# Attention blocks of 58 queries by 64 keys in batches 0 and 1, with v loaded by single heads

## The chip, the cores and the metric

The kernel runs on one core of a Trainium2 chip. The metric is the device time of one execution in microseconds (us). Several executions of a kernel are compared by their median.

## The reference

The program is an attention layer followed by a feed-forward layer. Attention has a local part, in which a position sees the keys less than four positions away, and a pooled part over averages of four positions:

```python
q_d = q.reshape(B, H, Sd, 4, D).mean(axis=3)          # B, H, S, D = 8, 8, 576, 64; Sd = 144
out_d = sm_attn(q_d, k_d, v_d)                        # softmax attention over all 144 averages
out_up = np.repeat(out_d, 4, axis=2)
mask = np.abs(pos[:, None] - pos[None, :]) < 4
scores = np.where(mask, scale * q @ k.T, -1e9)
attn_out = out_up + softmax(scores) @ v
x = attn_out.transpose(0, 2, 1, 3).reshape(4608, 512)
h = x @ w_in                                          # w_in: 512 x 2048
out = np.where(h > 0, h, np.exp(np.minimum(h, 0)) - 1) @ w_out
```

All inputs and the output are float32; the kernel's matmul operands are fp16.

## The kernel before

The eight batches each have four pairs of heads. A batch gives 576 of the 4608 rows of x, and the feed-forward layer works in nine blocks of 512 rows, so its block 0 needs batch 0 alone and block 1 needs batches 0 and 1.

For each pair (load, cast, transposes, scores, weigh): q and k come by DMA as float32, are cast to fp16 on DVE, POOL or ACT, and are transposed on TensorE by a matmul against an identity, with the averages of four beside them. DVE or ACT evicts the result into qt, kt and kd. In batches 0 and 1 (SIX) six neighbouring tokens lie in one partition, and k of some pairs comes as fp16 straight into a tile kc by a GpSimd DMA. In the other batches each partition holds one token of each 96-token block.

Local scores are made in small tiles. A block of 96 queries is two halves of KB = 48 queries, each against a window of KR = 64 keys; six blocks cover the 576 positions. Four such tiles (two halves, two heads) run in the four quarters of TensorE's array. One group for a pair is 24 of these matmuls (line 757) and 12 of 64 by 72 for the pooled scores. In batch 0 the mask is added by a matmul of NEG (line 763), in the others the exponentials are multiplied by MASK on DVE (line 792). ACT takes the exponential of a pair in one instruction (line 787).

The sums of the exponentials (denominators, line 810) are inverted by DVE (line 828) and spread over the partitions. In batches 0 and 1 (BY_PE) TensorE does that with a selection matrix (line 841) and DVE or ACT evicts it into rcb (line 850). In the others GpSimd writes them to DRAM and reads them back (lines 855 and 860).

v is loaded by load_v into the same windows: 64 partitions for each half, 48 blocks of 64 floats, in two DMAs per half (line 568; one of batch 0's by ACT, the others by SP). It is cast to fp16 (line 572) and pooled by matmuls (line 722 in batch 0, line 705 in the others), which are evicted into vd. The outputs (line 883) are again small tiles of 64 by 48 and 64 by 72. DVE normalizes them into xn (lines 910 and 914), and DVE or POOL adds the local and the repeated pooled part into xt (line 933), which is the x that the feed-forward layer reads.

In the feed-forward layer mm1 (line 950) makes 16 tiles of h for a block of 512 rows, four matmuls each. ACT and DVE apply the activation (lines 956, 958 and 961). mm2 (line 979) makes four output tiles in four parts each, ACT evicts them (line 995) and SP stores them (line 997). The weights come in eight parts by GpSimd DMAs (line 606).

The order is made in the kernel's Python. Each operation has an engine, an assumed duration and a rank. The class Plan plays these on the engines, gives out buffers and PSUM banks, and lets an engine take the ready operation of the lowest rank. The program is then written in that order, and every engine executes its own list strictly in order. The ranks come from the tables PARAM and FIRST, and PARAM also chooses engines (its e_ entries). WGATE and LGATE name an operation that a weight part, or a load of batch 1, waits for; the tiny memsets at line 1041 are these gates. While TensorE would stand idle early on, the plan inserts matmuls on a tile of zeros (fill, line 357). Eight semaphores serve the DMAs of SP and ACT in turn, so the ninth DMA waits for the first to land.

Of the kernel before, what the change touches and what calls it, by code (L numbers as in the profile page):

```python
# [12 lines left out]
AB = mybir.AluOpType  # L13
# [3 lines left out]
SD = S // 4  # L17
# [7 lines left out]
NR = 10  # L25
# [15 lines left out]
BY_PE = (0, 1)  # L41
WIC = (0, 512, 1024, 1536, 2048)
# [22 lines left out]
class Plan:  # L65
# [197 lines left out]
    def emit(self):  # L263
        for o in self.order:
# [8 lines left out]
PARAM = dict(e_d0=2, e_d1=0, e_d2=0, e_d3=1, M0=27.21, P=36.34, LAG=0.71, LEAD=52.25, GAP=6.32, SC=5.0,  # L273
             DEN=30.8, OUT=1.3, OUTG=2.09, LOAD=15.53, VLOAD=34.45, VCAST=9.57, warm=3.4, FILL=36.0, WI=-28.49,
             WO=59.77, WOG=5.01, OVER=1.64, LEAD1=58.97, GAP1=6.47, OUT1=55.0, VLOAD1=29.88, LOAD1=41.47,
             CC=-34.39, tv0=-22.07, C0=-2, SC0=3.1, OUTA=-23.54, OUTB=-20, DEN0=2.92, DENB=-27.58, SPA=-26.75,
             SPB=-20.86, V0=-43, G0=0, G1=0, G2=0, G3=2, G4=12, G5=6, G6=12, G7=3, G8=13, L0=0, L1=1, L2=2,
             L3=4, L4=4, LAG0=0.75, BY4=-51.82, TV1=0.68, C1=-19.87, e_cq0=0, e_cq1=1, e_cq2=1, e_cq3=1,
             e_ck0=0, e_ck1=0, e_ck2=1, e_ck3=1, e_q0=1, e_q1=0, e_q2=0, e_q3=0, e_k0=1, e_k1=1, e_k2=0,
             e_k3=0, QG=2.5, tvA=-26, e_v0=2, e_v1=1, e_v2=2, e_v3=1, e_g0=1, e_g1=1, e_g2=1, e_g3=1, e_r0=1,  # L280
             e_r1=0, e_r2=1, e_r3=1, e_xr0=0, e_xr1=1, e_xr2=0, e_xr3=1, e_a0=1, e_a1=0, e_a2=1, e_a3=0,
             e_xq0=1, e_xq1=0, e_xq2=1, e_xq3=0, e_xk0=1, e_xk1=0, e_xk2=1, e_xk3=1, KS=-64, KSG=3, e_s0=0,
             e_s1=1, e_s2=1, e_s3=0, e_xs0=0, e_xs1=1, e_xs2=1, e_w0=0, e_w1=1, e_w2=0, e_w3=0, e_xs3=0)

FIRST = {
    "add000": 0.72, "add001": 3.11, "add010": 0.8, "add011": 1.42, "add020": -0.47, "add030": 1.32,
    "add031": 0.68, "cast000": 0.77, "cast011": 1.41, "cast021": 4.15, "cast030": 0.71, "den00": -0.64,
    "den02": -0.88, "evk00": 0.17, "evk01": -0.98, "evk03": 0.21, "evq00": -5.46, "evq01": -5.01,
    "evq03": 0.38, "evr01": -3.98, "evr02": -2.25, "evv01": 6, "evv02": -2.4, "evv03": 0.21, "ex00": -5.19,
    "ex01": 5.05, "ex02": 0.83, "ex03": -1.67, "load00k": -4.99, "load01k": -2.41, "mask1": 6, "mask6": -3.11,  # L290
    "out00": -0.66, "out01": 4.25, "out02": -0.47, "out03": 1.13, "recip02": -2.47, "sc01": 0.78,
    "sc03": -0.22, "select": -0.15, "sixths": -1.87, "spr00": -2.79, "spr01": -3.25, "spr02": -1.4,
    "spr03": -1.43, "tens": 0.56, "tk00": -5.07, "tk01": -0.72, "tk02": 3.96, "tk03": 1.15, "tq00": 3.92,
    "tq01": 0.71, "tq02": -1.94, "tv00": -4.97, "vb": 1.68, "vc00": 2.37, "vc01": -3.26, "vc02": -4.17,
    "xn00": -1.03, "xn01": -5.03, "xn02": -0.06,
# [4 lines left out]
def kernel(  # L300
# [15 lines left out]
    def many(kind, shape, dt=FP16):  # L316
# [8 lines left out]
        "qt": many("qt", [128, 720]),  # L325
        "kt": many("kt", [128, S + 16]),
        "ex": many("ex", [128, 2, EW]),
        "vd": many("vd", [128, 3, NPAIR, 128]),
        "rcb": many("rcb", [128, NPAIR, 2, GW]),
        "rc": many("rc", [128, HD]),  # L330
        "xn": many("xn", [128, 2 * GW]),
# [32 lines left out]
    def const(name, shape):  # L364
# [4 lines left out]
        "BY6": const("BY6", [QB, NB, SD]),  # L369
        "VR": const("VR", [128, 32]),  # L370
        "VB": const("VB", [128, 28]),
        "BND": const("BND", [128, KR + KB]),
        "MASK": const("MASK", [128, NB, KB]),
        "NEG": const("NEG", [128, NB, KB]),
        "FIRST": const("FIRST", [128, 32]),
        "PICK": const("PICK", [128, 2, 51]),
        "EYE": const("EYE", [128, 128]),
# [718 lines left out]
```

## Time and profile before

| | |
|---|---|
| median of three runs | 349.6 us (348.94 to 353.46) |
| the profiled execution | 349.04 us |
| its span, first to last instruction | 347.3 us |
| granted TensorE clock, mean | 0.984 |
| instructions | 10965 |
| first feed-forward matmul | 34.12 us |

A profile's groups have this form: line, engine and operation, destination <- source, shape, count, then the busy time, the mean of one in ns, and the idle time before them with the releaser that ended most of it. In a timeline, a line has the start, the duration, the engine and the count, and in brackets the idle time ahead of it and what ended it. PEld is the loading of weights into TensorE, which runs beside its matmuls. "issue" is time for which the profile names no wait. The page's slices are fortieths of the span, 8.7 us each, and each digit is a busy share in tenths.

### The profile page before, as it was taken

Reading aid. Unit: us, or ns where it says so; the run is one execution under the profiler, and the core shown is the slowest. Engines: PE = TensorE matmul, PEld = TensorE weight load, DVE = VectorE, ACT = ScalarE, POOL = GpSimd, SP = SyncE. Lnnn points to the kernel's source line nnn. Section 1 sums busy time; section 2 is a strip of 40 time slices with the busy share of each in tenths; the row PEclk is TensorE's granted clock in tenths of the full one; section 3 lists DMA queues with packets and bytes.
Section 4 is the critical chain, followed back from the end, with each engine's and each line's share of the span. In section 5 each row is a group of like instructions: output and inputs, shape, how many; then the busy total and the mean of one; then the engine's idle time right before and its main releaser. Section 6 shows DMA issues by size and latency. Waiting matters only on the chain.

```text
span 347.3 us, 10965 instructions
## 1 busy us (share of the span) xinstructions
PE 331.9 (96%) x4672; PEld 172.4 (50%) x4672; DVE 218.0 (63%) x459; ACT 196.4 (57%) x337; POOL 132.6 (38%) x190
## 2 busy tenths in 40 slices
PE   6967999999999999899989999999999999999995
PEld 3744564555554455445544455545554444444443
DVE  6564788467474986377756786577657738655530
ACT  3582577297754686277817762776376325444431
POOL 6583133765449443732455246623410150000000
PEclk9896999999999999999999999999999999999999
DMA  8999999999999999999957995003100310001011
GB/s 204 208 213 243 195 191 205 176 192 233 223 186 202 237 227 224 178 244 216 192 131 141 189 202 137 32 32 87 64 32 30 90 64 30 32 30 60 32 54 67
DMA packets 120196, 49.73 MB, mean 143 GB/s; under 512 B 106996, under 2 KB 114708, under 8 KB 120148
## 3 DMA queue, kind: packets, MB, share of 16 engines
q1 hardware_dynamic: 112004, 39.33, 58.1%
q0 software_dynamic: 6592, 9.32, 14.5%
q8 instruction: 36, 0.59, 0.8%
q10 hardware_dynamic: 1552, 0.39, 0.6%
q14 instruction: 12, 0.10, 0.1%
HBM read 44.27 MB, written 9.55 MB: 155 GB/s over the span
## 4 chain that ended last, share of the span: by engine, by line
PE 58%; issue 0%; ACT 0%; DVE 0%; ACTq 0%
PE bank L979 27%; PE bank L950 24%; PE bank L662 2%; PE bank L883 2%; PE bank L757 1%; PE bank L705 1%; PE bank L810 1%; ACT os L995 0%; DVE xn L914 0%; ACTq L995 0%
## 5 line engine op out<-in xcount | busy, mean ns | idle before, releaser
L979 PE MATMUL bank<-WO,gt 128*128 128x512 f16 (+1 forms) x592 | 141.5, 374 | 1.5 <-DVE xn L914 1.2
L950 PE MATMUL bank<-xt,WI 128*128 128x512 f16 x576 | 141.6, 380 | 0.5 <-DVE gt L961 0.5
L956 ACT ACTIVATE e<-bank 128x512 f16<-128x512 f32 x144 | 86.8, 604 | 62.0 <-PE bank L950 45.1
L958 DVE TENSOR_SCALAR e<-e 128x512 f16<-128x512 f16 x144 | 58.0, 406 | 72.7 <-ACT e L956 72.5
L961 DVE SCALAR_TENSOR_TENSOR gt<-bank,e 128x512 f16<-128x512 f32 x144 | 98.6, 689 | 5.2
L979 PEld LDWEIGHTS <-gt 128*128 128x128 f16 x592 | 55.1, 98 | 60.4 <-DVE xn L914 1.7
L950 PEld LDWEIGHTS <-WI 128*128 128x128 f16 x576 | 53.5, 98 | 61.2 <-issue 2.9
L625 POOL CAST c<-ld 96x768 f16<-96x768 f32 x54 | 44.7, 839 | 34.5 <-issue 15.2
L933 POOL TENSOR_TENSOR xt<-xn 128x64 f16<-128x64 f16 (+7 forms) x62 | 40.4, 678 | 40.6 <-DVE xn L914 40.5
L995 ACT COPY os<-bank 128x512 f32<-128x512 f32 (+1 forms) x37 | 21.2, 575 | 40.9 <-PE bank L979 40.7
L910 DVE TENSOR_TENSOR xn<-bank,rcb 128x576 f16<-128x576 f32 x32 | 24.1, 753 | 22.0 <-POOL xt L933 9.8
L787 ACT ACTIVATE ex<-bank 128x1008 f16<-128x1008 f32 x32 | 31.6, 1010 | 8.3 <-PE bank L757 8.3
L572 POOL CAST v<-v 128x768 f16<-128x768 f32 x30 | 24.7, 848 | 23.1 <-DMA v<-in_v_dram 11.6
L677 ACT CAST qt<-bank 128x720 f16<-128x720 f32 x24 | 18.3, 763 | 18.6 <-PE bank L662 18.5
L662 PEld LDWEIGHTS <-c 96*128 96x128 f16 x288 | 18.9, 97 | 10.2 <-POOL c L625 0.5
L662 PE MATMUL bank<-ONE,c 96*128 96x120 f16 x288 | 22.1, 216 | 0.0
L855 POOL DMA_DIRECT2D rd<-rc x6 | 3.5, 579 | 47.2 <-DVE rc L828 44.7
L689 ACT CAST kt<-bank 128x576 f16<-128x576 f32 x24 | 15.8, 658 | 2.3 <-PE bank L662 2.3
L792 DVE TENSOR_TENSOR ex<-ex,MASK 128x576 f16<-128x576 f16 x28 | 14.9, 536 | 3.4 <-ACT ex L787 3.4
L883 PEld LDWEIGHTS <-v 64*64 64x64 f16 x768 | 9.4, 111 | 9.2 <-issue 9.1
L883 PE MATMUL bank<-ex,v 64*64 64x48 f16 x768 | 11.8, 191 | 1.8 <-issue 1.8
L757 PEld LDWEIGHTS <-kt 64*64 64x64 f16 x768 | 9.0, 109 | 8.0 <-issue 6.3
(90 smaller groups left out, 218.5 us busy)
## 6 DMA issues: line engine op xcount, KB each, us to landing
v<-in_v_dram SPq DMA_DIRECT2D x29, 384.0 KB, 7.7
ld<-in_q_dram SPq DMA_DIRECT2D x32, 288.0 KB, 6.0
out_dram<-os SPq DMA_DIRECT2D x35, 256.0 KB, 2.0
ld<-in_k_dram SPq DMA_DIRECT2D x28, 288.0 KB, 5.9
rcb<-rd POOLq DMA_DIRECT2D x12, 360.0 KB, 6.1
WI<-in_moe_w_in_dram POOLq DMA_DIRECT2D x4, 512.0 KB, 15.1
WO<-in_moe_w_out_dram POOLq DMA_DIRECT2D x4, 512.0 KB, 15.5
v<-in_v_dram SPq DMA_DIRECT2D x2, 368.0 KB, 8.5
```

The source lines that it names most:

```text
L572: f(out=at(x)[:, j].rearrange("p e c d -> p (e c) d"), in_=at(x32)[:, 12 * j : 12 * j + 12, :])
L625: f(out=at(y)[:], in_=at(x)[:].rearrange("p e c d -> p c e d"))
L662: nc.tensor.matmul(o, t[:, c, :, :], C["ONE"][:], start=True, stop=True)
L787: lambda: nc.scalar.activation(out=at(x)[:], in_=two(sc, 0, 128, 0, EW), func=AF.Exp, scale=SCALE),
L883: nc.tensor.matmul(PS[64 * e : 64 * e + 64, z.slot[0] + g, a : a + n], lhs, rhs, tile_position=(KR * r, 64 * e), **kw)
L910: nc.vector.tensor_tensor(out=_free(x, [[KB, 2], [QB, NB], [1, KB]]), in0=_free(zz, [[512 + HD, 2], *local]), in1=_free(yy, [[HB + SD, 2], ...
L933: f(out=at(xt(t))[:, j, o : o + n - a], in0=ln, in1=gn, op=AB.add)
L950: nc.tensor.matmul(one(h, 0, 128, 0, TBLK), WI[:, dc, 128 * fc : 128 * fc + 128], at(x)[:, dc, :], start=(dc == 0), stop=(dc == DMC - 1),)
L956: op("ACT", 0.55, r, lambda: nc.scalar.activation(out=at(e)[:], in_=one(h, 0, 128, 0, TBLK), func=AF.Exp), reads=[h], writes=[e], name=f"e ...
L958: op("DVE", 0.42, r, lambda: nc.vector.tensor_scalar(out=at(e)[:], in0=at(e)[:], scalar1=1.0, scalar2=-1.0, op0=AB.min, op1=AB.add), reads ...
L961: op("DVE", 0.64, r, lambda: nc.vector.scalar_tensor_tensor(out=at(gt)[:, fc, :], in0=one(h, 0, 128, 0, TBLK), scalar=0.0, op0=AB.max, in1 ...
L979: nc.tensor.matmul(one(z, 0, 128, cols.start, cols.stop), at(gt)[:, fc, 128 * tt : 128 * tt + 128], WO[:, fc, cols], start=(fc == 0), stop ...
```

## The change

Batches 0 and 1 take blocks of MP = 116 queries, two halves of MB = 58, each against the same window of 64 keys. Five blocks cover 580 positions, so that the last half has two pad columns more. A group of local scores is then 20 matmuls of 58 (the last four of 60) columns, a group of outputs 20 of 58. The pooled averages are laid out in halves of MU = 73 columns instead of 72, since 58 is no multiple of four. This needs its own constants for the mask (MASM, NEG), for pooling v (VB, VC, VM) and for the sums (PICK). v of these batches has 40 blocks instead of 48. As a block of 116 does not divide a head's 576 positions, one DMA takes one head: four DMAs for each half of two pairs where there was one. Four of batch 0's are issued by ACT, the others by SP.

PARAM and FIRST have new values throughout. Among them are the engines of casts and evictions, the pairs whose k comes by GpSimd, and the gates of the weights: the four parts of the output weights now all wait for casts of batch 1's v, and input weight parts 1 and 0 leave in that order. The order that results has, on TensorE, 37 fillers ahead of the first feed-forward matmul instead of 24, and none behind it instead of four. Scores of pair 0 of batch 1 and the transposes of its pair 1's q now stand ahead of that matmul. The order of the first operations on TensorE, before and after:

```
before: fill x10, q0 k0 transposed, fill x3, q1, scores 0, k1, q2, k2, scores 1, q3, k3, scores 2,
        denominators 0+1, v pooled (first half), scores 3, spread 1, 0, output 1, denominators 2+3,
        fill x2, v pooled (second half), output 0, spread 2, 3, fill x4, output 2, 3, fill x3,
        batch 1: q0, fill, k0, fill, first feed-forward matmul
after:  fill x15, k0, fill x4, q0, fill x9, q2, q1, fill, k1, fill x6, scores 0, 1, k2, q3, k3, fill x2,
        denominators 0+1, v pooled (second half), scores 3, 2, spread 0, v pooled (first half), spread 1,
        denominators 2+3, output 0, 2, spread 3, output 1, spread 2, output 3,
        batch 1: q0, k0, scores 0, q1, first feed-forward matmul
```

DVE, from the second reciprocal on, has normalization 0, addition 0, normalizations 1 and 2, the cast of q of batch 1's pair 1, normalization 3, the eviction of batch 1's k0, addition 3. POOL has the additions of pairs 1 and 2, with the cast of q of batch 1's pair 2 between them.

The core of the diff:

```diff
+MB, MP, MU = 58, 116, 73
+MW = 4 * MU
+MX = 5 * MP
...
+        def main_m(i, h, eng):
+            t = at(x32)[KR * h : KR * h + KR]
+            for e in range(2 * i, 2 * i + 4):
...
+                eng.dma_start(out=t[:, 5 * e + c0 : 5 * e + 5, :], in_=bass.AP(
+                    tensor=a.tensor, offset=a.offset + (e * S + MB * h - 3 + MP * c0) * D,
+                    ap=[[D, KR], [MP * D, 5 - c0], [1, D]]))
...
             def cast(j, eng):
+            if m:
+                f(out=at(x)[:, j, :, 0:5, :], in_=at(x32)[:, 10 * j : 10 * j + 10, :].rearrange("p (e c) d -> p e c d", e=2))
+                return
...
+            for i in range(5) if m else ():
+                n = MB if i < 4 else MB + 2
+                for h, e, p in tiles:
+                    t = MP * i + MB * h
+                    put(e, h, MB * i, n, kt[p, t : t + KR], qt[p, t : t + n], start=not hide, stop=not hide or i == 4)
...
-            for i in range(NB):
+            m = b in SIX
+            n, w, u = (MB, MW, MU) if m else (KB, HB, HD)
+            for i in range(5 if m else NB):
                 for h in range(2):
                     for e in range(2):
-                        put(h, e, h, HD * h + KB * i, KB, v_[half[h], j, e, i, :],
-                            ex[half[h], e, KB * i : KB * i + KB], start=True, stop=True)
+                        put(h, e, h, u * h + n * i, n, v_[half[h], j, e, i, :], ex[half[h], e, n * i : n * i + n],
+                            start=True, stop=True)
...
-    c_neg = op("DVE", 0.6, -54, lambda: nc.vector.tensor_scalar(
-        out=C["NEG"][:], in0=C["MASK"][:], scalar1=-1.0, scalar2=30000.0, op0=AB.add, op1=AB.mult), after=[c_mask], name="neg")
+    c_neg = op("DVE", 0.5, -54, ones_m, after=[c_em], name="neg")
...
+    c_vc = op("POOL", 0.74, -55, lambda: band(C["VC"][:], [[-4, 30]], 1, -5, 3), after=[o_clear], name="vcon")
+    c_vm = op("DVE", 0.5, -54, fours_m, after=[c_vb, c_vc], name="fours_m")
```

## The prediction, made before the changed kernel ran

> **What bounds the kernel now.** I read the page's busy shares and its forty slices first, then the chain of waits, then TensorE's timeline around its longest idle time, then the DMA queues in two windows there.
>
> ```profile
> PE 331.9 (96%) x4672; PEld 172.4 (50%) x4672; DVE 218.0 (63%) x459; ACT 196.4 (57%) x337; POOL 132.6 (38%) x190
> ...
> DMA  8999999999999999999957995003100310001011
> ```
>
> TensorE is the bound from its first feed-forward matmul on, and the DMA engines are full until about 180 us. So the question is when that first matmul starts, and what holds TensorE after it. The timeline of TensorE and the others from 18 to 35 us:
>
> ```profile
> 17.68 0.77 POOL L606 DMA_DIRECT2D WI<-in_moe_w_in_dram  x1
> ...
> 20.80 0.82 POOL L572 CAST v<-v 128x768 f16<-128x768 f32 x1 [0.47 <-DMA v<-in_v_dram]
> ...
> 28.08 0.21 PE L841 MATMUL bank<-rc,SEL 32*128 32x72 f16 x1 [4.47 <-issue]
> 28.33 0.76 ACT L850 CAST rcb<-bank 128x720 f16<-128x720 f32 x1 [2.94 <-PE bank L841]
> 30.99 0.76 DVE L910 TENSOR_TENSOR xn<-bank,rcb 128x576 f16<-128x576 f32 x1 [2.71 <-PE bank L883]
> ...
> 34.12 1.03 PE L950 MATMUL bank<-xt,WI 128*128 128x512 f16 x4
> ```
>
> The last matmul of the spreading of batch 0 (line 841) stands 4.47 us idle, for "issue": no semaphore is named, its weights are loaded, its operands are old. The eviction at 28.33, the normalization at 30.99 and the first feed-forward matmul at 34.12 follow from it one after another. What it waits for shows in the DMA queues of 20 to 25.4 us and of 25.4 to 28.1 us:
>
> ```profile
> q0 software_dynamic: 731, 0.73, 88.5%
> ```
>
> ```profile
> q8 instruction: 1, 0.02, 2.3%
> ```
>
> In the first window the software queue (the weights that GpSimd issued from 16.91 on) fills the engines and no packet of the instruction queue q8 moves; in the second one does, and TensorE goes on. The page gives q8 36 packets and 0.59 MB, 16.4 kB each, and TensorE has 9344 loads and matmuls: one packet per 260. Counted in order in the trace, TensorE's pauses that no semaphore explains begin after instructions 957, 3516, 4540, 5564 and 6588 (4.67, 0.57, 1.58, 1.30 and 0.49 us), which lie 2559, 1024, 1024 and 1024 apart, multiples of 256. I read these as waits for the next block of 256 instructions, with edges at 189, 445, 701, 957, 1213 and so on. One of them in the page's manner, inside a group of equal matmuls:
>
> ```profile
> 174.59 0.32 PE L883 MATMUL bank<-ex,v 64*64 64x48 f16 x18
> 176.02 0.24 PE L883 MATMUL bank<-ex,v 64*64 64x48 f16 x6 [1.12 <-issue]
> ```
>
> From the moment an edge is crossed until the next block but one can be used took 3.3 to 3.7 us for the first two edges, 8.1 us for the block used at 28.08, about 6 us for the two after it. Where POOL's spreading transfers (line 860) were in flight, it took 6 to 9 us (98.0 to 106.7, 132.7 to 140.6, 168.8 to 176.0, 204.7 to 211.2).
>
> **The change part by part.** The profiled execution took 349.04 us, its span is 347.3; the median of the runs is 349.6. I sum against 349.04, so 1.74 us lie around the span.
>
> Matmuls of batches 0 and 1: a score group has 24 of 48 columns, then 16 of 58 and 4 of 60, 1152 against 1168 columns; the row at 16.75 gives 0.21 us for its 24. Pooled ones grow from 72 to 73 columns. By columns that is +1.4% on 16 groups of 0.21, under 0.1 us: nothing. There are 64 matmuls less, so 128 instructions less to fetch. Exponentials go from 1008 to 1022 elements (1010 ns each, +0.014), evictions, masks and normalizations by 1 to 2%: eight of each, about 0.2 us on ACT and DVE beside TensorE. If that cover is gone, 0.2 us.
>
> Transfers of v: 48 blocks become 40, so 1.57 MB a batch becomes 1.31. The three transfers of batch 0 on SP landed 2.05 us apart in the median of their 16 parts, 188 GB/s, so 1.4 us of DMA time per batch, 2.8 in all. Casts of v shrink from 826 ns to about 690. Against that, SP issues 13 transfers for v of batch 0 in place of 4 and 16 in place of 4 for batch 1, at 0.31 to 0.60 us where the queue had room: 5 and 6 us more on SP. Transfers queued behind them: batch 1's q and k, and batch 2's. SP stood 3.1 us at 4.41 for a landing already, and each small transfer (82 kB) takes 0.44 us at 188 GB/s, so eight in flight hold 3.5 us of work: I take the queue as full, cost nothing; bound 0 to 2 us. ACT issues four transfers at the start where it issued one (0.74 us): up to 2.2 us more, hidden before its first copy at 5.86. The new constants cost DVE some ten memsets and copies of 0.06 to 0.25 us and POOL three selections of about 0.25; DVE's first cast starts near 5 instead of 4.05, and SP's first q lands at 6.5: hidden. With v ending nearer 18.5 than 20.67, 2 us would come free.
>
> The order takes them back. In the changed kernel 37 fillers instead of 24 stand ahead of the first feed-forward matmul, the scores of pair 0 stand after three more transposes and six fillers, scores 3 and 2 stand behind the pooling of v's second half, and ACT casts v twice before its first exponential. With durations of the rows: cast of k1 waits for q2's landing (11.6) and ends at 13.3; eviction of q0 on DVE ends near 15.9; scores 0 at 16.0 to 16.8 (they were at 11.0); ACT's casts of v until 17.1, two exponentials until 19.1; first denominators 19.7; pooling 20.6; scores 2 and 3 until 22.1; last exponential 23.8; second denominators 24.6 (they were at 20.4). From there DVE has one reciprocal, four normalizations, a cast, a key eviction and two additions, 7.9 us: 32.5. Later still are loads: queries of pairs 1 and 2 of batch 1 are let go by DVE only after the second pooling's eviction, at 24.2. In the trace of before such a load took 7 to 9 us (23.39 to 30.64, 18.64 to 27.7). DVE's cast of the one stands ahead of the fourth normalization, POOL's cast of the other ahead of an addition that the first feed-forward matmul needs. 24.4 + 7 + 3.8 (cast, normalization, eviction, addition) gives 35.2. Weights: the first feed-forward matmul's part leaves POOL behind two casts of v, near 20 instead of 16.91; it took 11.1 us, so it lands at 31, hidden by the 35.2. The output weights all leave behind the casts of batch 1's v. They are wanted about 18 us after the first feed-forward matmul (584 instructions, at the 33 per us of 34 to 59 us). Two fewer parts (3.4 us each) and less v lie ahead of them, so I cost them at nothing, with a bound of 3 us. So without any wait for instructions the first feed-forward matmul starts at 35.2, against 34.1.
>
> Now the blocks. Edges 701 and 957 fall into the pooling of v's first half and into output 1; edge 1213 falls six instructions ahead of the first feed-forward matmul, which stood at 1169, before that edge. Edge 445 is crossed near 19, when GpSimd's first weight transfer (issued near 16.9) moves. At 3.3 us the next block is there at 22.5, no wait; at 8.1 us it comes at 27. I take 6.3, the nearest rows being those of 28 to 41 us: 25.3, 2.6 us late. That moves the loads behind it: 35.2 + 2.5 = 37.7. The blocks of edges 957 and 1213 come at 25.3 + 6.3 = 31.6 and at 37.9, which leads to the same time. Between 35.2 and 37.7 I take 37.0, nearer to the late end, because the weights are moving by then as they were before the 4.47 us.
>
> The rest: before, 347.3 - 34.12 = 313.2 us. Scores 0 and queries 1 of batch 1 have moved ahead of that matmul (0.38 and 0.64), four fillers are gone (0.86): 311.3. Of the four later block waits (3.9 us), batch 2's spreading now meets an edge 282 instructions after its denominators, with the next one 538 after. At 15 us after the denominators the instruction is wanted; before, a block asked for in that window came 19.4 us after. So about 4 us there; 2 for batch 3, whose edge lies at the window's beginning; batches 4 and 5 ask earlier, nothing. 6 against 3.9: +2. The bounds are -3.9 and +6, from no wait at all and from 4 us for batches 2 and 3 each and 2 for batch 4. 37.0 + 311.3 + 2 + 1.7 = 352.0.
>
> The Trainium skill ("Runtime: NRT & Kernel Launch", section "Instruction fetch mechanics") says that instructions come in 16 KiB blocks of 256, agreeing with the 16.4 kB per packet here. It also says that crossing a block is mostly hidden and gives TensorE room for 2048 instructions; the 4.47 us here speak against both. By its rule the sum would be that of rival 1.
>
> **The rivals.** 1. No block comes late. For it: 30 of 36 blocks came in time; edge 445 may be crossed before the weights move. Against: between edges 189 and 957 the trace of before lost 0.5 and 4.67 us. Then 35.2 + 311.3 - 3.9 + 1.7 = 344.3; if the loads also land in 5 us, as the first of batch 1 did (16.9 to 21.6), 342.3. 2. On the other side: TensorE is starved three times running. If each block after edge 445 takes 8.1 us, as the one used at 28.08 did, edge 701 passes at 27, 957 at 35, 1213 at 43.4; with +2 later, 43.4 + 311.3 + 2 + 1.7 = 358.4. It decides from about 7.5 us a block on: 19 + 3 x 7.5 = 41.5, and with the rest 356.5. 3. The v transfers do not get shorter because SP's issuing (0.5 us each, 13 of them) takes as long as what is saved: v lands at 20.7 as before. The first half's casts, and the pooling behind them, move by up to 2 us: 354.
>
> **How the numbers follow.** My forecast has a chance of 0.55 (own range 348 to 356), rival 1 0.22, rival 2 0.17, rival 3 0.06. Of rival 1 a quarter lies under 342.6, which is 2% faster and about what a measurement of this kernel can tell from no change: 0.06. Of rivals 2 and 3 0.17 lie over 356.6. Within 2%: 0.77. The range of 344 to 359 leaves out half of rival 1 and a little above.
>
> **What would show it.** Right: the first feed-forward matmul (line 1030 of the changed file) at 35 to 39 us, with idle time for "issue" in the pooling of v's first half (line 788) or in output 1 (line 959); pauses at multiples of 256 from 189; one of about 4 us some 15 us after batch 2's denominators. Wrong: v's last transfer after 20 us; the first feed-forward matmul before 34 us; no pause at an edge before 40 us; or a wait for the output weights near 55 us.

## The result, and the profile after

The changed kernel takes 361.3 us (median of 6 executions, 359.2 to 365.6); the kernel before took 350.7 on the same chip (6 executions). The ratio is 1.0285, 95% interval 1.022 to 1.035: slower, and outside the forecast range of 344 to 359. The profiled execution took 362.56 us: 43.80 to the first feed-forward matmul (forecast 37.0), 317.1 from there to the end of the span (forecast 313.3), 1.7 around the span. So 6.8 us of the miss lie ahead of that matmul and 3.8 behind it. Ratios here and below leave out executions more than 1.5% above the fastest of the same kernel, which matters for e9, where six of ten are left out (by the medians of all, its ratio is 1.020), and for the profiled executions of e8 and e9, which are among those left out.

The page of the changed kernel: busy TensorE, the granted clock, the DMA engines, and the chain of waits.

```profile
PE 341.0 (95%) x4605; PEld 178.6 (49%) x4605; DVE 211.4 (59%) x476; ACT 196.2 (54%) x337; POOL 133.2 (37%) x195
...
PEclk9985589999999899999999999999999999999999
DMA  8759889999999999999994988413010311001012
...
PE 76%; DMA 12%; SPq 4%; DVE 2%; issue 2%; POOL 1%; ACT 1%; ACTq 0%; POOLq 0%
PE bank L1059 33%; PE bank L1030 30%; DMA v<-in_v_dram 8%; PE bank L722 4%; SPq L622 3%; PE bank L959 3%; DMA WO<-in_moe_w_out_dram 2%; PE bank L823 2%; DMA ld<-in_k_dram 2%; PE bank L886 1%; PE bank L771 1%; PE bank L917 1%; DVE e L1038 1%
```

The DMA engines were full at the start of the kernel before (8999...); now there is a dip to 5 in the third slice. The chain of waits names v's transfers (8%) and SP's issuing of them at line 622 (SPq, 3%). And the clock is at half in slices four and five and in parts of three and six (24.0 to 47.8 us). SP's list in the first 22 us shows the place:

```profile
4.77 1.20 SPq L581 DMA_DIRECT2D ld<-in_q_dram  x2
9.89 0.29 SPq L619 DMA_DIRECT2D v<-in_v_dram  x1
10.23 11.48 SPq L622 DMA_DIRECT2D v<-in_v_dram  x12
```

In the kernel before, SP issued the three large ones like this:

```profile
7.55 6.92 SPq L568 DMA_DIRECT2D v<-in_v_dram  x3
```

In the changed kernel SP stands until 9.89, when the second of the four small transfers that ACT issued has landed (the semaphores go round in turn), and then needs 11.5 us for 12 transfers. In the chain each of them takes 0.62 us at SP, and the last one 4.17 us from its issue to its landing at 23.82:

```profile
12.65 0.04 issue
12.70 0.62 SPq L622
13.32 0.04 issue
13.37 0.62 SPq L622
...
19.64 4.17 DMA v<-in_v_dram
```

82 kB every 0.66 us is 124 GB/s; by the prediction's figure the larger transfers before had moved at 188 GB/s. The DMA engines' share and the bytes tell the same. These are stretches of ten us: length, busy time and count of each engine, granted clock, DMA share, GB/s.

```profile
10.00:20.00 10.00, 8.63 (x179) 6.01 (x176) 2.85 (x5) 5.27 (x9) 3.00 (x7) 1.00 0.85 156
20.00:30.00 10.00, 6.37 (x147) 3.66 (x144) 3.47 (x9) 3.24 (x7) 2.07 (x3) 0.70 0.64 104
30.00:40.00 10.00, 7.86 (x207) 6.92 (x204) 6.57 (x15) 3.13 (x5) 6.97 (x10) 0.50 0.95 202
```

The kernel before moved 206 and 225 GB/s in the first two. In the second stretch batch 1's loads are missing too: their gates open only when v's second half is pooled, and SP issues the first of them at 26.41. From v on, the timeline of the changed kernel goes like this:

```profile
24.97 0.80 PE L788 MATMUL bank<-v,VM 128*32 128x256 f16 x9 [3.63 <-POOL v L629]
...
35.19 0.32 PE L959 MATMUL bank<-ex,v 64*64 64x58 f16 x8 [1.73 <-issue]
...
38.68 1.72 DVE L685 CAST c<-ld 96x768 f16<-96x768 f32 x1 [0.39 <-PE bank L705]
...
40.33 0.74 DVE L990 TENSOR_TENSOR xn<-bank,rcb 128x580 f16<-128x580 f32 x1
...
42.01 0.48 PE L823 MATMUL bank<-qt,kt 64*64 64x58 f16 x20 [2.16 <-DVE kt L745]
...
43.80 1.48 PE L1030 MATMUL bank<-xt,WI 128*128 128x512 f16 x3
```

TensorE waits 3.6 us for the cast of v's second half; then an edge of a block of 256 instructions (in output 1, as forecast; after instruction 959 by count, where the forecast had 957) costs 1.7 us. Last comes a row of single steps: transposes of queries 0 of batch 1, a cast on DVE that can only start when these have left its buffer, the fourth normalization behind the cast in DVE's list, the key eviction, scores 0, transposes 1, and only then the first feed-forward matmul. Later, in batch 2, there is the other pause that was forecast, 15.1 us behind the start of its denominators and nine blocks of 256 behind the first one; batch 3 has none:

```profile
116.16 0.30 PE L959 MATMUL bank<-ex,v 64*64 64x48 f16 x6 [3.11 <-issue]
```

### The profile page after: what moved, and what is told of

Read it like the earlier page. It is cut to its first block, busy times and chain, and to the rows that moved or that the text cites. A ratio compares the mean times of both kernels' runs of the same rounds, so it can differ in the third digit from the quotient of the medians.

```text
span 360.9 us, 10889 instructions
## 1 busy us (share of the span) xinstructions
PE 341.0 (95%) x4605; PEld 178.6 (49%) x4605; DVE 211.4 (59%) x476; ACT 196.2 (54%) x337; POOL 133.2 (37%) x195
## 4 chain that ended last, share of the span: by engine, by line
PE 76%; DMA 12%; SPq 4%; DVE 2%; issue 2%; POOL 1%; ACT 1%; ACTq 0%; POOLq 0%
PE bank L1059 33%; PE bank L1030 30%; DMA v<-in_v_dram 8%; PE bank L722 4%; SPq L622 3%; PE bank L959 3%; DMA WO<-in_moe_w_out_dram 2%; PE bank L823 2%; DMA ld<-in_k_dram 2%; PE bank L886 1%; PE bank L771 1%; PE bank L917 1%; DVE e L1038 1%; PE bank L788 0%; POOL v L629 0%
## 5 line engine op out<-in xcount | busy, mean ns | idle before, releaser
L1030 PE MATMUL bank<-xt,WI 128*128 128x512 f16 x576 | 140.0, 382 | 0.6 <-DVE gt L1041 0.4
L1038 DVE TENSOR_SCALAR e<-e 128x512 f16<-128x512 f16 x144 | 51.8, 362 | 72.3 <-ACT e L1036 71.7
L1030 PEld LDWEIGHTS <-WI 128*128 128x128 f16 x576 | 54.3, 98 | 64.1 <-issue 4.4
L1059 PEld LDWEIGHTS <-gt 128*128 128x128 f16 x592 | 55.3, 98 | 59.8 <-issue 3.8
L685 POOL CAST c<-ld 96x768 f16<-96x768 f32 x57 | 46.8, 836 | 31.6 <-DMA ld<-in_q_dram 14.1
L990 DVE TENSOR_TENSOR xn<-bank,rcb 128x576 f16<-128x576 f32 (+1 forms) x32 | 24.1, 754 | 32.1 <-PE bank L959 24.0
L858 ACT ACTIVATE ex<-bank 128x1008 f16<-128x1008 f32 (+1 forms) x32 | 31.4, 1015 | 9.6 <-PE bank L823 9.6
L631 POOL CAST v<-v 128x768 f16<-128x768 f32 x24 | 19.4, 836 | 5.2 <-DMA v<-in_v_dram 4.2
L931 POOL DMA_DIRECT2D rd<-rc x6 | 3.5, 581 | 47.6 <-DVE rc L904 23.8
L959 PE MATMUL bank<-ex,v 64*64 64x48 f16 (+1 forms) x736 | 11.8, 194 | 4.8 <-issue 4.8
L823 PEld LDWEIGHTS <-kt 64*64 64x64 f16 x736 | 8.9, 111 | 10.2 <-issue 6.7
L823 PE MATMUL bank<-qt,kt 64*64 64x48 f16 (+2 forms) x736 | 11.2, 193 | 2.2 <-DVE kt L745 2.2
```

The lines of the kernel that those rows point to most:

```text
L685: f(out=at(y)[:], in_=at(x)[:].rearrange("p e c d -> p c e d"))
L823: nc.tensor.matmul(PS[KR * h : KR * h + KR, z + e, a : a + n], lhs, rhs, tile_position=(64 * e, KR * h), **kw)
L858: lambda: nc.scalar.activation(out=at(x)[:, :, 0:w], in_=two(sc, 0, 128, 0, w), func=AF.Exp, scale=SCALE),
L959: nc.tensor.matmul(PS[64 * e : 64 * e + 64, z.slot[0] + g, a : a + n], lhs, rhs, tile_position=(KR * r, 64 * e), **kw)
L990: nc.vector.tensor_tensor(out=_free(x, [[n, 2], [2 * n, c], [1, n]]), in0=_free(zz, [[512 + u, 2], *local]), in1=_free(yy, [[k + 2 * u, 2] ...
L1030: nc.tensor.matmul(one(h, 0, 128, 0, TBLK), WI[:, dc, 128 * fc : 128 * fc + 128], at(x)[:, dc, :], start=(dc == 0), stop=(dc == DMC - 1),)
```

## Experiments

Every run was timed against the kernel before on its own chip. The table gives the ratio of the times with its 95% interval and, of the profiled execution, when v of batch 0 had wholly landed, when the first feed-forward matmul (FFM) began, and for how long TensorE's clock was at half. A stretch of half clock that the end of the span cuts off is not counted. Executions of one kernel differ by up to some 5 us and each row's profile is of a single one, so a difference of one or two us between two FFM columns is not a finding by itself; from the profiles of e8 and e9 only places and landings are read. With the new blocks, a transfer of two or four heads (e1, e5, e9, e10, e12, e14, e15) uses one stride, so some heads get other rows than the attention needs: these kernels measure time and are no way to mend the change.

| run | v of batches 0 and 1 by | ratio | v landed | FFM | half clock |
|---|---|---|---|---|---|
| before | four heads | 1 | 20.7 | 34.1 | 10.2 |
| the changed kernel | one head | 1.0285 (1.022 to 1.035) | 23.8 | 43.8 | 27.3 |
| e1, old way of loading | four heads | 1.0226 (1.019 to 1.027) | 20.7 | 39.9 | 13.7 |
| e2, before with single heads | one head | 1.0238 (1.020 to 1.028) | 31.6 | 40.7 | 13.7 |
| e3, new blocks, old order | one head | 1.0201 (1.014 to 1.026) | 26.3 | 38.2 | 17.1 |
| e4, old blocks, new ranks | four heads | 1.1172 (1.111 to 1.123) | 22.1 | 41.6 | 37.5 |
| e5, new blocks alone | four heads | 1.0020 (0.999 to 1.005) | 19.0 | 34.5 | 6.8 |
| e6, weight part behind the casts | one head | 1.0318 (1.027 to 1.036) | 23.9 | 41.3 | 17.1 |
| e7, fillers at the pooling | one head | 1.0302 (1.023 to 1.038) | 22.6 | 42.1 | 13.7 |
| e8, edges 128 earlier | one head | 1.0329 (1.025 to 1.041) | 23.0 | 42.3 | 27.3 |
| e9 | two heads | 1.0121 (1.007 to 1.018) | 21.3 | 40.0 | 17.1 |
| e10, e1 with the part behind the casts | four heads | 1.0139 (1.007 to 1.021) | 18.3 | 40.6 | 13.7 |
| e11, before, edges 184 earlier | four heads | 1.0038 (0.999 to 1.008) | 21.2 | 35.9 | 13.7 |
| e12, batch 1 alone by four | one / four | 1.0257 (1.019 to 1.032) | 23.4 | 41.5 | 13.7 |
| e13, cast behind the normalization | one head | 1.0364 (1.033 to 1.040) | 24.4 | 40.5 | 23.9 |
| e14, e10 and the cast behind | four heads | 1.0163 (1.010 to 1.022) | 18.3 | 35.7 | 13.7 |
| e15, e10 and the cast by ACT | four heads | 1.0195 (1.013 to 1.026) | 17.8 | 36.5 | 17.1 |
| e16, the cast by ACT | one head | 1.0407 (1.036 to 1.045) | 22.5 | 40.0 | 17.1 |
| e17, four more issued by ACT | one head | 1.0335 (1.025 to 1.042) | 22.8 | 40.3 | 13.7 |
| e18, e13 and output weights early | one head | 1.0259 (1.016 to 1.036) | 22.9 | 38.4 | 23.9 |

### The three parts of the change, one at a time

The theory after the changed kernel's trace was: the single-head transfers cost SP's queue more than they save, and the new order costs the rest; the blocks themselves cost nothing. The rival was that the order alone costs everything. e1 keeps the changed order and blocks, with the old four heads in one DMA:

```diff
-            for e in range(2 * i, 2 * i + 4):
-                eng.dma_start(out=t[:, 5 * e + c0 : 5 * e + 5, :], ...
+            eng.dma_start(out=t[:, 5 * e + c0 : 5 * e + 20, :], ...   # uniform stride of blocks
```

> The changed kernel with v of batches 0 and 1 in one transfer for four heads again (20 blocks at one stride of 116 tokens, so the rows of all heads but the first of each four are not the ones that attention needs; sizes, packets and the orders on all engines stay). Theory S (supply: small transfers and the waits of SP between them leave the DMA engines short): v of batch 0 ends by 19.5 us instead of 23.8, the first feed-forward matmul moves from 43.8 to about 37, and the time from 361 to about 354. Theory O (order: the order alone is slow, whatever the transfers): v may land earlier, but the time stays at 359 to 361.

Measured 356.55 us, between the two theories: v landed at 20.69 and the first feed-forward matmul came at 39.9. Against the kernel before on its own chip that is 1.0226 instead of 1.0285, and the intervals overlap: this pair by itself does not show a gain. e2 does the opposite in the kernel before:

```diff
+            for c in range(c0 - c0 % NB, c1, NB):     # batches 0 and 1: one head's blocks
+                eng.dma_start(out=t[:, max(c, c0) : c + NB, :], in_=blocks(max(c, c0), c + NB, KB * h - 3, KR))
```

> The kernel before with nothing changed but that v of batches 0 and 1 comes in one transfer per head (6 blocks each, 98 kB), issued by the same engines in the same places. S: SP needs about 0.66 us for each of 12 transfers and waits for landings ahead of them, so v of batch 0 ends at 24 to 25 us instead of 20.7 and the time is 354 to 357 against 350.7. O: v is not what matters, within 1 us of before.

Measured 357.31, 8 us slower than before from this alone. v landed at 31.62: the weights that GpSimd issued at 16.87 to 19.06 took the DMA engines from small transfers that SP had still to issue. e3 takes the changed kernel with PARAM and FIRST of the kernel before, e4 the kernel before with those of the changed one:

> Blocks of 58 by 64 and single-head transfers of the changed kernel, with all the ranks, engines and gates of the kernel before. S: like the kernel before with single heads, 353 to 357. O: 349 to 351, as before.

> Blocks of 48 by 64 and v's transfers of the kernel before (four per batch), with the ranks, engines and gates of the changed kernel. S: about 354 to 356, since the transfers are large again and only the order's own cost of some 4 us (scores behind the pooling, later gates) is left. O: 359 to 361.

e3 measured 355.97, as expected. e4 measured 390.28, outside both expectations, and told nothing of the parts: with the old blocks these ranks give another plan, 346 us long behind its first feed-forward matmul, with the clock at half in six stretches. e5 is e3 with e1's way of loading, so of the change only the blocks are left:

> The changed kernel with v of batches 0 and 1 moved four heads in one transfer (from a uniform stride, so three of four heads read other rows) and with the order of the kernel before: of the change only the blocks of 58 by 64 are left. If the cost lies in the single-head transfers and in the order, and the blocks cost nothing: 347 to 351 us, first feed-forward matmul at 33 to 34.5, v landed at or before 20.7. If the blocks themselves cost: 353 or more, with longer DVE or ACT work ahead of that matmul.

Measured 350.88, ratio 1.002 (0.999 to 1.005): to within half a per cent the blocks cost nothing and gain nothing. Between e5 and e3 only the single heads differ, and that is 1.8%, 6.3 us of 350. In the changed order, the five runs with two or four heads at once have ratios of 1.012 to 1.023 (mean 1.017), the eight with all single heads 1.026 to 1.041 (mean 1.032): 1.6%, 5.5 us. The two ranges do not overlap. The pairs that differ in the heads alone scatter: 1.8% between e6 and e10, whose intervals lie apart, and 0.6% between the changed kernel and e1.

### Is it the number of transfers, SP's issuing, or the DMA engines?

> The changed kernel with v of batches 0 and 1 moved two heads in one transfer (from a uniform stride, so every second head reads other rows): half as many transfers, each 164 kB. If SP's 0.66 us from issue to issue is the bound of the 82 kB transfers, it is none any more at 164 kB (249 GB/s, above the 188 GB/s that the engines moved): v's last landing near 20.7 to 21.5 as with four heads, 356 to 358 us. If the cost goes by the number of transfers alone, half of the 4.8 us is left: v near 22.3, 359 us.

```diff
-            for e in range(2 * i, 2 * i + 4):
+            for e in (2 * i, 2 * i + 2):              # 10 blocks each
```

Measured 357.17, ratio 1.0121 (1.020 by all executions), no worse than four heads. A transfer of 164 kB takes SP 0.64 us to issue, like one of 82 kB, and SP's seven were out by 14.1. v landed at 21.3: half as many transfers took away 2.5 of the 3.1 us that lie between single heads and four heads (e1), not half of them. That is what a bound by the time from issue to issue gives, since twice the bytes go in the same 0.66 us. e6 leaves the small transfers and takes away what shares the DMA engines with their end, the weight part that GpSimd issued at 13.60 and not, as forecast, at 16.9:

```diff
+    first = next(o for o in plan.order if o.name == "w1")
+    plan.order.remove(first)
+    plan.order.insert(1 + next(i for i, o in enumerate(plan.order) if o.name == "w0"), first)
```

> The changed kernel with the weight part that GpSimd issues at 13.6 us put behind the casts of v's second half and behind the other first part. If v is late because that weight part takes DMA engines from its last transfers: v's last landing at 21.5 to 22.5 instead of 23.8, the first feed-forward matmul near 42, 358 to 360 us. If only SP's issuing of small transfers bounds v: last landing at 23 to 23.8, 361 us. If the part is then missed later: a wait of TensorE for it behind the first feed-forward matmul.

Measured 361.27. SP still took until 19.39 to issue and the last transfer's 16 parts landed at 21.77 in the median (23.35 in the changed kernel), though one part came at 23.86. From 12 to 22 us the DMA engines were busy for 0.34 to 0.54 of the time, in stretches of two us (1.03 to 1.42 in the kernel before): they waited for SP. So SP's issuing is a bound by itself, near 21.8. e17 takes away the other one, with four of the transfers moved to ACT, which stands idle there, and the weight part left where it was:

```diff
+    o = plan.order.pop(at_("vm02"))
+    o.eng, o.fn = "ACT", lambda f=o.fn: f(eng=nc.scalar)
+    plan.order.insert(1 + at_("evk00"), o)
```

> The changed kernel with four more of the single-head transfers of batch 0's v (first half of the blocks, heads 4 to 7) issued by ACT, behind its key eviction near 9 us, where it stood idle until 13.8; SP issues the other nine. If SP's 0.66 us from issue to issue bounds v: SP's last issue near 17 instead of 19.6, v's last landing near 21.5 instead of 23.8, the first feed-forward matmul 2 us earlier, 357 to 360 us. If the DMA engines, with the weight part among them, bound it: 23 to 24 as before, 361 us.

Its timeline, SP, ACT and GpSimd side by side:

```profile
11.57 5.28 SPq L622 DMA_DIRECT2D v<-in_v_dram  x7
12.22 5.08 ACTq L622 DMA_DIRECT2D v<-in_v_dram  x4
...
13.95 0.78 POOL L666 DMA_DIRECT2D WI<-in_moe_w_in_dram  x1
```

The last transfer is issued at 16.70 instead of 19.64, but the last landing is at 22.84, only 1.0 us earlier: what is issued after 13.95 shares the engines with the weight part, and landed at 19.3 or later. ACT, busy with issuing until 17.3, came to its casts of v's first half at 18.75 instead of 16.00, a cost that this run brings in itself. 361.04 us: no gain. The Trainium skill ("DMA: Bandwidth & Descriptors", section "Issuing engines are not separate DMA queues") says that issuing from several engines saves only the time it takes to initiate a DMA, which it calls usually small beside the DMA itself. The first half agrees with this run (2.9 us of issuing saved, 1.0 us of landing); the second does not hold for these transfers, whose 0.66 us at SP is longer than the 0.44 us that 82 kB take at the 188 GB/s of the larger ones. e10 takes away both bounds at once, large transfers and the weight part behind the casts:

> The kernel with v in transfers of four heads (uniform stride, so three of four heads read other rows), and besides the weight part that GpSimd issued at 12.9 us put behind the casts of v's second half. This is what the forecast had assumed of v and of that part: v then lands near 18.5, the first feed-forward matmul starts at 37 to 38 and the time is 352 to 354 us. If v lands near 18.5 and the matmul stays near 40, the order's own chain was forecast too short: 356 us. If v stays near 20.5, that part was not what held it.

v landed at 18.30, where the forecast had it (18.5). The time was 355.49, 1.4% above before. So v is late for two reasons, one behind the other: with large transfers alone it had wholly landed at 20.7 (e1), with the weight part moved alone at 23.9 (e6), with both at 18.3. But v on time does not bring the forecast's 352.

e12 asks whether batch 1's single heads cost anything of their own:

```diff
+            n = 1 if b == 0 else 4
+            for e in range(2 * i, 2 * i + 4, n):
```

> The changed kernel with v of batch 1 alone in transfers of four heads (uniform stride, three of four heads of batch 1 read other rows); v of batch 0 as in the changed kernel. If the single-head transfers of batch 1 cost time of their own (they hold SP from 43 to 55 us, and the output weights behind the casts): first feed-forward matmul at 43.8 as in the changed kernel, waits for the output weights near 71 to 78 us gone, 358 to 360 us. If batch 0's alone cost: 361 us.

Measured 358.67, ratio 1.0257 (1.019 to 1.032) against the changed kernel's 1.0285 (1.022 to 1.035). It points the way of a cost in batch 1, and the wait for the output weights at 71 us is gone, but the intervals overlap: how the 5.5 us divide between the two batches is not settled.

### What holds the first feed-forward matmul once v is there

In e10 v was 5.5 us earlier than in the changed kernel and the matmul only 3.2. Its timeline shows why:

```profile
33.04 1.32 POOL L1012 TENSOR_TENSOR xt<-xn 128x512 f16<-128x512 f16 x2
...
33.20 4.04 DVE L684 CAST c<-ld 96x768 f16<-96x768 f32 x1 [0.66 <-DMA ld<-in_q_dram]
34.31 0.81 POOL L684 CAST c<-ld 96x768 f16<-96x768 f32 x1
35.09 1.05 POOL L1012 TENSOR_TENSOR xt<-xn 128x512 f16<-128x512 f16 x1
```

DVE's cast of queries 1 takes 4.04 us beside GpSimd's casts and additions; at 27.72 in the kernel before, where GpSimd stood idle, a cast of the same size took 0.56. The fourth normalization stands behind it. e13 moves it out of the way in the changed kernel, e14 in e10, and e15 and e16 give it to ACT:

```diff
+    for x, y in (("cast110", "add030"), ("tq11", "mm1_0_0")):     # e13, e14
+        o = plan.order.pop(at_(x))
+        plan.order.insert(1 + at_(y), o)
```

```diff
+    o.eng, o.fn = "ACT", lambda f=o.fn: f(eng="ACT")               # e15, e16: cast110
```

> The changed kernel with two operations moved: DVE's cast of queries 1 of batch 1 behind the fourth normalization, the key eviction and the last addition ahead of the first feed-forward matmul, and TensorE's transposes of these queries behind that matmul. If the chain transposes of queries 0, cast (1.72 us), normalization, key eviction, scores, transposes 1 (1.3 us) is what holds the first feed-forward matmul once v's chain is through: it starts 2.5 to 3 us earlier, near 41, and the time falls by 1 to 2.5 us to 359 to 360. If TensorE is bound by something else there: 43.8 and 361.

> The kernel with v in transfers of four heads (three of four heads read other rows) and the first weight part behind v's casts, and besides the two operations moved behind the fourth normalization and behind the first feed-forward matmul. v lands at 18.3 and the chain is shortened: the first feed-forward matmul near 37 and 352 to 353 us if these three are what the forecast had wrong ahead of that matmul; 355 if the time is lost elsewhere.

> The kernel with v in transfers of four heads (three of four heads read other rows) and the first weight part behind v's casts, with DVE's cast of queries 1 of batch 1 done by ACT instead. On DVE it took 4.04 us while GpSimd ran a cast, additions and a transfer's issue, and 0.56 to 0.75 us alone. If DVE was held up by GpSimd's work: on ACT near 0.8 us, the fourth normalization 2 to 3 us earlier, the first feed-forward matmul near 38, 353 us. If the cast was long for its data: as long on ACT, and 355 us.

> The changed kernel with DVE's cast of queries 1 of batch 1 done by ACT instead. The cast took 1.72 us on DVE and stood ahead of the fourth normalization: the first feed-forward matmul 1 to 1.7 us earlier, 359 to 361 us.

The first feed-forward matmul came at 40.5 and 40.0 (from 43.8), and at 35.7 and 36.5 (from 40.6). With v on time the chain does hold it: with the cast away it is where the forecast had it, at 37.0 or before. With v late the step is less sure, since other kernels that keep the cast (e6, e7, e8, e12, e17) have it at 40.3 to 42.3. On ACT the cast took 0.84 us beside the same work of GpSimd, from the timeline of e15:

```profile
33.43 0.84 ACT L684 CAST c<-ld 96x768 f16<-96x768 f32 x1
33.49 0.81 POOL L684 CAST c<-ld 96x768 f16<-96x768 f32 x1
34.27 1.05 POOL L1012 TENSOR_TENSOR xt<-xn 128x512 f16<-128x512 f16 x1
```

So on DVE the cast was long because of what GpSimd did beside it, not for its data. The Trainium skill ("SBUF — State Buffer", section "Who interferes with whom") states this as a rule: a DVE cast in a 2-port mode and a GpSimd instruction lock each other out for whole instructions, and ACT waits for no one. The 4.04 us on DVE and 0.84 on ACT agree with it; which mode the cast ran in, no run here shows.

But the times didn't follow: 361.2 (e13) and 363.2 (e16) us against 361.3, by ratio even 1.036 and 1.041 against 1.0285, and 355.3 (e14) and 355.6 (e15) against 355.5. In the profiled executions most of the earlier start was given back before 146 us; from TensorE's instruction 4028 on, all of these kernels take 214.6 to 214.8 us. One place is seen. In TensorE's waits from 44 to 120 us, the line for the output weights grew; first the changed kernel, then e13:

```profile
PE bank L1059 <- DMA WO<-in_moe_w_out_dram: 1.3, 1, 1.3
```

```profile
PE bank L1059 <- DMA WO<-in_moe_w_out_dram: 2.5, 1, 2.5
```

e18 issues the first two output parts early, behind the last input part:

```diff
+    for x, y in (("w4", "w2"), ("w5", "w4")):
+        o = plan.order.pop(at_(x))
+        plan.order.insert(1 + at_(y), o)
```

> The changed kernel with the cast and the transposes moved behind the fourth normalization and the first feed-forward matmul (which alone brought that matmul from 43.8 to 40.5 us and the time to 361.2), and besides the first two parts of the output weights issued by GpSimd right behind the last part of the input weights, ahead of the casts of batch 1's v. If what the earlier matmul had won was given back to the wait for the output weights (2.58 us at 67.9): that wait is gone and the time is 358 to 359 us, or batch 1's v comes late instead. If it was lost elsewhere: 361 us.

360.72 us. The wait shrank to 0.8 us, and a wait of 1.9 us for a GpSimd cast of batch 2 came in its place; batch 1's v was not late (landed at 59.8 us, at 62.5 in e13). In the changed kernel the DMA engines are full from slice 7 to slice 21 (54 to 190 us): it may be that what is loaded earlier makes something else later there, but beyond this one wait no run shows it.

### The clock and the blocks

> The changed kernel with the first 19 of its fillers moved to just ahead of the pooling of v's second half, so that TensorE works through the wait for v at 21 to 25 us. The instruction count at every later place is as before. If the half clock of 24 to 48 us is what this wait sets off and it costs time by itself: full clock through 25 to 45 us, the first feed-forward matmul 1.5 to 3 us earlier, 357 to 359 us. If TensorE is bound by waits there and the clock costs nothing: 360 to 362 us.

361.8 us. The half clock came later and for half as long (32.8 to 46.4 instead of 24.0 to 47.8), and the profiled execution took 357.58, but the median did not move. The interval, 1.023 to 1.038, leaves room for 2 to 3 us either way.

> The changed kernel with 32 of its fillers written as three matmuls each on a third of the columns: the same columns, 128 instructions more ahead of the first feed-forward matmul, so every later edge of 256 instructions falls 128 instructions earlier in the work. If the waits for no semaphore are waits for the next block: the 1.98 us in output 1 and the 3.33 us of batch 2's spreading leave those instructions; batch 2's edges fall 154, 410 and 666 instructions behind its second denominators instead of 26, 282 and 538, and the wait there is 0 to 1.5 us; 356 to 359 us. If these waits belong to the instructions they are seen at, both stay: 361 us.

The waits for no semaphore in the changed kernel (first line) and in e8:

```profile
PE bank L959 <- issue: 4.8, 2, 3.1
```

```profile
PE bank L961 <- issue: 3.4, 2, 2.6
PE bank L1061 <- issue: 2.2, 1, 2.2
PE bank L707 <- issue: 2.1, 1, 2.1
```

The pause of batch 2 is gone, as expected, and pauses stand at other operations (transposes, a matmul of the second feed-forward part, a local output), after instructions 959, 1215, 5567 and 6591 of its own count: 959 plus multiples of 256. The waits go with the count and not with the operation. Their sum, 7.7 us against 4.8 in these two executions, is no finding; the median was 362.5, not the 356 to 359 that was expected. e11 does the same to the kernel before:

> The kernel before with its 24 fillers written as four or five matmuls each on a part of the columns: the same columns, 184 instructions more at the start, so every edge of 256 instructions falls 184 instructions earlier in the work. If the pauses are waits for blocks: none of 4.67 us in the spreading of batch 0, those of 1.58 and 1.30 us leave their instructions, and others may come at the new edges; 7 to 8 us of pauses in all against 8.6, 347 to 351 us. If the pauses belong to their instructions, they stay where they are in the work.

The 4.67 us in batch 0's spreading and the 1.58 and 1.30 us later are gone; 2.93 and 1.45 us, counted in the same way from start to start, stand after instructions 957 and 1213, in other operations. Time the same, 1.0038. Shifting the edges moved these waits and did not remove them.

No run beat the kernel before; e5 and e11 equal it.

## Why the prediction was wrong, point by point

**v's transfers: the step that failed.** "I take the queue as full, cost nothing; bound 0 to 2 us." SP's 0.31 to 0.60 us an issue were counted, and hidden behind eight transfers in flight. They were not hidden: 0.66 us from issue to issue is longer than the transfer itself (0.44 by the step's own figure), so the DMA engines are busy for only 0.33 of the time from 12 to 14 us, and the queue starts late, at 9.9, because SP's turn at the semaphores waits for ACT's small transfers among the queries and keys. v came at 23.82 instead of 18.5, past the 20 us that the prediction had named as its sign of being wrong. Rival 3 had the mechanism and the place, at less than half the price: it let v land at 20.7 and took 354. The single heads cost 1.6 to 1.8%, 5.5 to 6.3 us (e1, e9, e10, e14, e15 against the rest; e5 against e3; e10 against e6), more than half of the 2.85%. Two numbers in the step should have warned: with 0.5 us an issue, 82 kB go at 164 GB/s, below the 188 that the large ones made.

**The first weight part near 16.9.** It went at 13.60, ahead of the casts. Alone this cost nothing that can be measured (e6), but it is the second bound of v (e17).

**The order's chain: right start, wrong middle.** The pooling of v's second half was to come at 20.6 and came at 24.97, 4.4 of the 6.8 us. From there to the first feed-forward matmul the forecast had 16.4 us and the trace 18.8. Left out were scores 0 and transposes 1 of batch 1, which the new order puts between the fourth normalization and that matmul: the forecast took their 1.0 us off the rest and never put it on the head, nor the wait in front of scores 0 (2.2 us in the changed kernel). The cast, 0.56 and 0.64 us in the kernel before, took 1.72 here and 4.04 in e10. The half clock, 23.9 us from 24.0 on, was in no term.

**Blocks.** Edge 957 in output 1: forecast, and there with 1.73 us. About 4 us in batch 2, 15 us behind its denominators: there with 3.11. Batch 3, forecast 2 us: none. e8 and e11 show that the waits go with the count of instructions; that it is a block's packet they wait for is read from the DMA queues. Not only GpSimd's queue delays that packet: ahead of the pause in output 1, from 28.9 to 32.4 us, SP's transfers held the engines for 78% and GpSimd's for 24%, and no instruction packet moved. Rival 2 gave 358.4 from three such waits in a row; it came nearest the measured time by a cause that did not occur.

**Output weights at nothing, bound 3 us.** They cost 1.3 us in the changed kernel and 2.5 in e13; the bound held, the value did not.

**The blocks of 58 at nothing.** Right: 1.002 in e5.

**What stays open.** With v landing where it was forecast and the chain shortened, the first feed-forward matmul is at 35.7 to 36.5 and the profiled execution of e14 takes 352.55, near the forecast's 352.0, but partly by chance (the matmul comes 1.3 us before the forecast's 37.0, and the rest takes 315.1 us instead of 313.3); that kernel's other executions took 354.9 to 359.3, and its median is 355.3. What the others lose is in no trace here, but the granted clocks are on record: 0.980 and 0.981 at 352.55 and 354.89 us, 0.971 at 355.75 and 359.27. That the DMA engines are full to 190 us and that an earlier start is given back to other loads was shown for one wait (e13, e18) and is argued for the rest. What the half clock costs by itself was not separated: 3.4 us of it cost at most 1.7 us, and the changed kernel has 17.1 us more of it than the kernel before in the profiled executions, but e7 nearly halved it without a gain in the median. An estimate from the granted clocks on record, with 2 x (1 - clock) x span as the half clock of one execution: among the 84 executions behind the ratios (the changed kernel and the experiments), 1 us more of it goes with 0.2 us more time of the same kernel. The changed kernel's median is 26 us of half clock, that of the kernel before 10 to 13, so some 3 of the 10 us may go with the clock. Whether the clock is the cause there or the waits that go with it, no run separates.

## What to carry to other kernels

Splitting a transfer is free only while each part still takes the DMA engines longer than the issuing engine: compare the time from issue to issue with bytes over the rate that the trace shows, and where the first is longer, count the issues one after the other on the path. When several bounds of one size stand in a row (issuing, a shared engine, a chain behind), a single experiment that removes one will read as "no effect"; remove them together before calling one innocent. An earlier start of the main work need not be a gain, as e13 and e16 show: follow it to the point from which both kernels take the same time.

## What the runs showed of the hardware that was not expected

- SP took 0.59 to 0.67 us to issue a transfer of rows of 256 bytes where it did not have to wait, whether it carried 82 kB (the changed kernel), 164 kB (e9) or 393 kB (0.60 us at 24.79 in the kernel before); ACT 0.64.
- Small transfers that were issued one at a time lost against GpSimd's large ones: v of the kernel before with single heads landed at 31.6 instead of 20.7 (e2), and 82 kB issued at 13.97 beside a weight part landed at 19.71 in the median of its parts (e18).
- DVE's cast of 96 x 768 elements took 0.56 us where GpSimd stood idle and up to 4.04 beside GpSimd's casts and additions; ACT's beside the same, 0.84.
- The clock's half stretches lasted 3.41, 6.83, 10.2, 13.65, 17.1 or 23.9 us, multiples of 3.41. In the changed kernel the longest began at 24.0, 2.6 us after the wait for v began (21.3), and went on through ten us in which TensorE was busy for 7.86.
- The granted clock differs between executions of one kernel: 0.962 to 0.985 in six of the changed kernel.
